# Two values of two products and two joined gates in the third blocks of batches 2 to 5

## The chip, the core and the metric

The kernel runs on one core of one Trainium2 chip. The core has a matrix engine (TensorE, PE in the profile), a vector engine (VectorE, DVE), a scalar engine (ScalarE, ACT), a general engine (GpSimd, POOL) and a queue engine for transfers (SyncE, SP). Each engine works through its own list of instructions in order; semaphores order the engines among each other. TensorE writes its products into PSUM, which here holds eight banks of 128 x 512 fp32. The metric is device time in microseconds (us) of one execution.

## The reference

For each of 8 batches of 3008 rows and 256 columns the real part of a two-dimensional Fourier transform is taken, and its rows go through a gated layer:

```python
X = np.fft.fft(x, axis=1)
X = np.fft.fft(X, axis=2)
x = X.real.reshape(B * S, D)
gate = np.maximum(x @ w_gate, 0.0)     # 256 -> 1536
val = x @ w_val                        # 256 -> 1536
out = gate * val @ w_out               # 1536 -> 256
```

## The kernel before, in words

**Mirror pairs.** The kernel folds the transform along the columns into the weights, and uses that the rows of a real transform come in mirror pairs. For a pair the gate (and the value) has the form A + B for the one row and A - B for its mirror. A is a product of the cosine parts `us` with WA, plus a term of channel 128 that is the same in both; B is a product of the sine parts `vs` with WB. Row 0 of `vs` carries channel 128 too, and row 0 of WB its weights. WM is -2 WB with row 0 set to zero, and `WV` is -0.5 WM, so WB with row 0 zero. Batch 0 is done in another way (`single_tile`, `first_tile`) that the change does not touch.

**Blocks, tiles and slots.** In batches 1 to 7 the pairs of a batch are cut into three blocks of 512, 512 and 481 columns (`thirds`, line 734). A block has 12 feature tiles of 128 features (fi = 0 to 11). One call of `slot` (line 1054) issues the work around one tile, `cur`; three further tiles are at earlier stages: `mid` (the next one), `nxt` (the one after it) and `after`. `pending` is the tile before `cur`. The slot whose `cur` is tile c is called slot c here; in it `pending` is tile c - 1, `mid` c + 1, `nxt` c + 2, `after` c + 3. The order of every engine's work is the order in which the kernel issues it (`manual_schedule`).

An ordinary tile goes through these steps:

- seed (`seed`, line 1014): ScalarE writes the channel 128 term of the gate into a p bank (two of them).
- sine and cosine of the gate (lines 1019 and 1026): TensorE makes -2B in the g bank, which ScalarE copies to q (line 1022), and adds the cosine product to the seed in the p bank, which gives A.
- `both` (lines 1030, 1031): VectorE makes A + B from q and the p bank; GpSimd then makes A - B from that and q. Both lie in SBUF, in buffers of tag r.
- value (`value`, lines 876 and 877): two products make A + B of the value in a v bank (two of them).
- first product (line 912, `relu_mult`): VectorE takes relu of the plus gate times the value and writes the first half of h.
- `mirror` (line 882): TensorE adds WM times `vs` to the same v bank, which turns it into A - B. It has to wait until VectorE has read the bank for the first product.
- second product (line 912, by `second`): VectorE makes the other half of h from the minus gate. For a block of 481 columns `keep_rest` (line 907) then copies 66 columns of h to `LB` by a DMA on the SP queue.

So an ordinary tile takes five products on TensorE and three operations on VectorE. The order inside a slot is, on TensorE: sine of `nxt`, some output products, cosine of `nxt`, mirror of `pending`, two value products of `cur`, more output products. On VectorE: second product of `pending`, first product of `cur`, `both` of `nxt`. On ScalarE: copy of q for `nxt`, seed of `after`, at most one eviction.

**Output products** (line 784) of the block before, 96 in a block of 512, fill the slots: `outs` of them in a slot, 8 in a third block, five eighths of them between sine and cosine and the rest behind the value. Every 24 of them make a PSUM bank full, which ScalarE copies out (line 797, the list `evict`: one entry of it is issued in each slot). **Transform products** (line 589) of the next batch go to the d bank during the first two blocks (`DFT_EVEN`). **Folds** of a later batch run on GpSimd, issued by a credit of 0.72 us in each slot (`run_fold`).

**Values of two products.** In the last third block of batch 6 and in batch 7 some tiles (`SHORT`, line 996) are marked `short`. For these ScalarE seeds the d bank with the channel 128 term of the value (`seed_value`, line 1035, at the end of the slot in which the tile is `nxt`). A slot later TensorE adds the cosine product (line 1039) and ScalarE copies twice that, 2A, to `a` (line 1040). A slot later again TensorE adds the sine product with `WV` (line 1044), so that the bank holds A + B, and VectorE makes the first product from it (line 912, reading d). In the slot after that VectorE takes 2A minus the bank, A - B, into `a` (line 1049) and GpSimd multiplies it by the minus gate (line 1050), on which ScalarE has done the relu (line 1103). There is no mirror product for such a tile. A `short` tile takes away two output products of the slot in which it is `mid` and adds one in each of the two slots after that.

**`widen`** (line 568) writes, by a product without a start flag, those columns of a bank that a transform product of 376 or 377 columns leaves out, so that a seed that ScalarE writes there is added to by the next product. It is issued for the transform of batch 7, which runs in batch 6. At batch 5, slot 0, a DMA on the SP queue (line 1210) sets row 0 of WB[0] to that of WM[0], zero.

Of the kernel before, what the change touches and what calls it, by code (L numbers as in the profile page):

```python
# [15 lines left out]
ALU = mybir.AluOpType  # L16
# [18 lines left out]
def kernel(  # L35
# [8 lines left out]
    nc = tc.nc  # L44
    B, S, D = x.shape
# [23 lines left out]
    WB = [single(f"WB{i}", [128, DF], BF16) for i in range(2)]  # L69
# [500 lines left out]
    def family(b, dst, fam, sine, now=True, pool=None):  # L570

        n, cols = (NE, slice(0, NE)) if fam == 0 else (NJ, slice(NE, NK))
        src, tab = (GG[b % 2], tabS) if sine else (FF[b % 2], tabC)
        st, apart = {}, now or pool is not None

        def mm(par, t, nyq=False):
            if par not in st and not apart and not par:
                st[0] = st[1]  # L580
            elif par not in st:
                home, tag = pool or ((psG, "g") if now and not par else (psD, "d"))
                st[par] = home.tile([128, 512], F32, name=tag, tag=tag)
            rows = slice(0, ROWS[par][t])
            if nyq:
                nc.tensor.matmul(st[par][0:1, 0:n], lhsT=FF[b % 2][rows, fam, t, par, 128:129], rhs=tabC[rows, 2 * t + par, cols],
                                 start=False, stop=(t == 2), skip_group_check=True)
            else:
                nc.tensor.matmul(st[par][:, 0:n], lhsT=src[rows, 1 - fam if sine else fam, t, par, 0:128],  # L589
                                 rhs=tab[rows, 2 * t + par, cols], start=(t == 0 and (apart or par == 1)), stop=(t == 2),  # L590
                                 skip_group_check=not apart)
                if (b, fam, sine, par, t) == (B - 1, 0, False, 0, 2):
                    widen(st[par], n)

        def end(par):
            if par:
                st["es"] = rp.tile([128, NE], F32, name="es", tag="es", bufs=2)
                evict.insert(0, lambda: nc.scalar.copy(st["es"][:, 0:n], st[1][:, 0:n]))
            elif not apart:
                whole, rest_ = half_of(dst, fam)  # L600
                evict.insert(0, lambda: nc.scalar.copy(whole, st[1][:, 0:n]))
                for c in (slice(0, NJ // 2), slice(NJ // 2, NJ)):
                    sums.append(lambda c=c: nc.vector.scalar_tensor_tensor(rest_[:, c], in0=st["es"][:, c], scalar=2.0, in1=st[1][:, c],
                                                                           op0=ALU.mult, op1=ALU.subtract))
            else:
                for d, op in zip(half_of(dst, fam), (ALU.add, ALU.subtract)):
                    m = d.shape[-1]
                    sums.append(lambda d=d, op=op, m=m: nc.vector.tensor_tensor(d, st["es"][:, 0:m], st[0][:, 0:m], op=op))
            if now:
                flush()  # L610

        def at(par):
            home, tag = pool
            st[par] = home.tile([128, 512], F32, name=tag, tag=tag)
            return st[par]
        return mm, end, at
# [242 lines left out]
    def run_one(todo):  # L859
        if todo:  # L860
            todo.pop(0)()
# [25 lines left out]
    def space():  # L887
        return rp.tile([128, 512], F32, name="r", tag="r", bufs=12)
# [26 lines left out]
    def second(st):  # L915
        (relu_mult if "s" in st else mult)(st, 1)
        if st["n"] == 481:
            keep_rest(st)
# [79 lines left out]
    def new_tiles():  # L998
        for b in range(1, B):
            for blk, block in enumerate(thirds):  # L1000
                for fi in range(NF):
                    st = tile_of(block, fi, uv[b])
                    st["b"] = b
                    st["kind"] = "o" if (b, blk, fi) == (1, 0, 6) else "n"
                    st["short"] = (b, blk) in ((6, 2), (7, 0), (7, 1)) and fi in SHORT or (b, blk) == (7, 2) and fi in (2, 5, 8)
                    st["lead"] = (b, blk, fi) == (1, 0, 0)
                    yield st

# [15 lines left out]
    def cosine_part(st):  # L1024
        n = st["n"]
        nc.tensor.matmul(st["p"][:, 0:n], lhsT=WA[0][:, st["f"]], rhs=st["us"], start=False, stop=True, skip_group_check=True)  # L1026

    def both(st):
        n, (q, sp, sm) = st["n"], st["s"]
        nc.vector.scalar_tensor_tensor(sp[:, 0:n], in0=q[:, 0:n], scalar=-0.5, in1=st["p"][:, 0:n], op0=ALU.mult, op1=ALU.add)  # L1030
        nc.gpsimd.tensor_tensor(sm[:, 0:n], sp[:, 0:n], q[:, 0:n], op=ALU.add)  # L1031

    def seed_value(st):
        st["v"] = bank("d")
        nc.scalar.activation(st["v"][:, 0:st["n"]], st["c"], ACTF.Copy, scale=b2[:, NF + st["fi"]:NF + st["fi"] + 1])
# [10 lines left out]
    def value_second(st):  # L1046
        n = st["n"]
        a = st["a"][:, 0:n]
        nc.vector.tensor_tensor(a, a, st["v"][:, 0:n], op=ALU.subtract)
        nc.gpsimd.tensor_tensor(half_h(st, 1), st["s"][2][:, 0:n], a, op=ALU.mult)  # L1050
        if n == 481:
            keep_rest(st)

    def slot(cur, mid, nxt, after, outs, fold_us):

        outs += cur["short"] + (pending is not None and pending.get("short", False)) - 2 * (mid is not None and mid["short"])
        stop = len(todo_out)

        def out(part):
            run(todo_out, len(todo_out) - stop + outs * part // 8)  # L1060
        old = nxt is not None and nxt["kind"] == "o"
        new = nxt is not None and nxt["kind"] == "n"
        if old:
            gate(nxt)
        lead = cur["lead"]
        out(4 if lead else 0)
        if new and mid["kind"] != "o":
            sine_part(nxt)
        out(4 if lead or nxt is None else 5)
        if new and mid["kind"] == "o":  # L1070
            sine_part(nxt)
        if new and not lead:
            cosine_part(nxt)
        if not lead:
            seed(after)
        if pending is not None and pending.get("short"):
            value_second(pending)
        elif pending is not None:
            mirror(pending["v"], pending, 1)
            second(pending)  # L1080
        if cur["short"]:
            value_sine(cur)
        else:
            value(cur)
        if mid is not None and mid["short"]:
            value_cosine(mid)
        if cur["kind"] == "o":
            mult(cur, 0, cur["first"])
        else:
            relu_mult(cur, 0)  # L1090
        if lead:
            out(5)
            cosine_part(nxt)
            seed(after)
        if new:
            both(nxt)
        if old:
            nxt["first"] = nxt["r"]
            mirror(nxt["g"], nxt, 0)
            relu(nxt)  # L1100
        if cur["short"]:
            sm = cur["s"][2][:, 0:cur["n"]]
            nc.scalar.activation(sm, sm, ACTF.Relu)
        if nxt is not None and nxt["short"]:
            seed_value(nxt)
        run_fold(fold_us)
        run_one(evict)
        run_one(sums)
        out(8)
        return cur  # L1110
# [4 lines left out]
    for b in range(B):  # L1115
# [4 lines left out]
        for blk, block in enumerate(blocks):  # L1120
# [72 lines left out]
            else:  # L1193
                for fi in range(NF):
                    at = NF * blk + fi
                    cur = ahead.pop(0)
                    add_h(cur, hs)
                    ahead.append(next(tiles, None))
                    outs = per_tile + ((-2, 0, -2, 2, 2, 0)[fi % 6] if per_tile == 7 else 0)
                    if (b, blk) == (B - 1, 2) and fi > 8:  # L1200
                        outs = (10, 9, 19)[fi - 9]
                        if fi == 9:
                            rest = out_steps(b, block, hs)
                            early, rest = rest[:10] + rest[12:16], rest[10:12] + rest[16:]
                            todo_out += early
                    if (b, at) in ((2, 5), (2, 9), (2, 13)):
                        f = slice(128 * (at - 5), 128 * (at - 1))
                        nc.scalar.mul(WV[:, f], WM[1][:, f], -0.5)
                    if (b, at) == (5, 0):
                        nc.sync.dma_start(out=WB[0][0:1, :], in_=WM[0][0:1, :])  # L1210
                    pending = slot(cur, *ahead, outs, .72)
                    for step in more_1.get(at, ()) if b == 1 else ():
                        step()
                    run(todo_dft, DFT_1[at] if b == 1 else DFT_EVEN[at])
# [44 lines left out]
```

## Time and profile before

| what | value |
|---|---|
| median of 3 runs | 626.28 us (626.09 to 626.63) |
| the profiled execution: time | 626.3 us |
| the profiled execution: span, first to last instruction | 624.5 us |
| mean granted TensorE clock | 0.999 of full speed |
| VectorE busy | 549.0 us (88%) |
| ScalarE busy | 464.3 us (74%) |
| GpSimd busy | 516.5 us (83%) |

A row of the timeline gives the start and the duration in us, the engine, the line and operation, and out<-in with partitions x elements; x3 means that three such instructions in a row are merged, and the duration is then from the start of the first to the end of the last. A bracket at the end tells how long the engine stood idle before it and what released it. Matmuls overlap: the next starts before the end of the one before is written, so what a product costs TensorE is the distance to the next start, not its duration.

### The profile page before, as it was taken

To read this page: it belongs to the slowest core of one execution; us is meant where nothing else is said; L and a number is where in the kernel's file an instruction comes from. 1 tells how busy PE (TensorE), PEld (TensorE's weight loads), DVE (VectorE), ACT (ScalarE), POOL (GpSimd) and SP (SyncE) were. 2 spreads that over 40 slices of the span, in tenths; PEclk is the share of its full clock that TensorE was granted. 3 is DMA by queue.
4 is the path that set the end of the run, shared out by engine and by line. 5 is a ranking of instruction groups with operands and counts; after the bars stand their busy time and mean duration, and the time that the engine had idled before them with its cause. 6 is when DMAs were issued, how large, how long until landed. Compare 5 with 4: busy or idle time off the path is not lost.

```text
span 624.5 us, 12395 instructions
## 1 busy us (share of the span) xinstructions
PE 615.7 (99%) x4047; PEld 397.1 (64%) x4091; DVE 549.0 (88%) x978; ACT 464.3 (74%) x854; POOL 516.5 (83%) x490
## 2 busy tenths in 40 slices
PE   8999999999999999999999999999999999999997
PEld 2566666566666666666666666666666666666666
DVE  8886677999899899988999999899999999999991
ACT  7796667777777767777777777777777768999982
POOL 8988992998899988799979989799896656888881
PEclk9999999999999999999999999999999999999999
DMA  9955758734264427315362425211211111211113
GB/s 241 212 199 132 176 186 105 186 64 143 86 153 141 133 70 198 101 48 163 85 189 66 138 77 127 57 52 51 77 47 52 43 61 37 61 52 51 44 52 104
DMA packets 86035, 66.48 MB, mean 106 GB/s; under 512 B 41639, under 2 KB 69063, under 8 KB 85970
## 3 DMA queue, kind: packets, MB, share of 16 engines
q1 hardware_dynamic: 81384, 60.02, 35.1%
q0 software_dynamic: 3984, 4.92, 4.0%
q8 instruction: 32, 0.52, 0.4%
q10 hardware_dynamic: 602, 0.75, 0.3%
q14 instruction: 33, 0.27, 0.1%
HBM read 41.89 MB, written 34.17 MB: 122 GB/s over the span
## 4 chain that ended last, share of the span: by engine, by line
PE 95%; DVE 1%; issue 1%; POOL 1%; DMA 1%; ACT 0%; DVEq 0%; POOLq 0%; ACTq 0%
PE o L784 38%; PE v L877 10%; PE v L882 10%; PE g L1019 9%; PE p L1026 8%; PE v L876 8%; PE d L589 4%; PE p L882 1%; PE p L876 1%; PE p L877 1%; DMA XG<-in_x_dram,gidx 1%; PE o L427 1%; POOL XG L120 1%; PE g L589 0%; DVE h L912 0%
## 5 line engine op out<-in xcount | busy, mean ns | idle before, releaser
L1031 POOL TENSOR_TENSOR r<-r 128x512 f32<-128x512 f32 (+1 forms) x251 | 312.6, 1253 | 84.3 <-DVE r L1030 83.1
L912 DVE SCALAR_TENSOR_TENSOR h<-r,v 128x512 bf16<-128x512 f32 (+1 forms) x478 | 303.5, 675 | 38.1 <-PE v L882 28.9
L784 PE MATMUL o<-wo,h 128*128 128x256 bf16 x2172 | 330.8, 272 | 0.2
L784 PEld LDWEIGHTS <-h 128*128 128x128 bf16 x2220 | 216.6, 98 | 111.5 <-issue 0.9
L1014 ACT ACTIVATE p<-CB,b 128x512 f32<-128x512 bf16 (+1 forms) x251 | 172.0, 685 | 62.3 <-DVE r L1030 61.2
L1022 ACT COPY r<-g 128x512 f32<-128x512 f32 (+1 forms) x251 | 144.8, 577 | 56.1 <-PE g L1019 51.0
L1030 DVE SCALAR_TENSOR_TENSOR r<-r,p 128x512 f32<-128x512 f32 (+1 forms) x251 | 168.5, 671 | 0.8 <-ACT r L1022 0.8
L877 PE MATMUL v<-V,WB 128*128 128x512 bf16 (+3 forms) x281 | 103.0, 367 | 2.1
L1019 PE MATMUL g<-V,WM 128*128 128x512 bf16 (+1 forms) x251 | 94.1, 375 | 0.2
L1026 PE MATMUL p<-U,WA 128*128 128x512 bf16 (+1 forms) x251 | 94.1, 375 | 0.0
L882 PE MATMUL v<-V,WM 128*128 128x512 bf16 (+1 forms) x240 | 89.9, 374 | 0.3 <-DVE h L912 0.2
L876 PE MATMUL v<-U,WA 128*128 128x512 bf16 (+3 forms) x245 | 89.3, 365 | 0.0
L901 DVE TENSOR_TENSOR h<-r,v 128x376 bf16<-128x376 f32 (+2 forms) x90 | 46.2, 547 | 16.4 <-PE v L882 10.5
L876 PEld LDWEIGHTS <-WA 128*128 128x128 bf16 x336 | 32.7, 97 | 37.3 <-issue 12.2
L797 ACT COPY os<-o 128x512 f32<-128x512 f32 x92 | 52.5, 571 | 2.9 <-issue 2.9
L877 PEld LDWEIGHTS <-WB 128*128 128x128 bf16 x336 | 32.7, 97 | 32.3 <-ACT WB L680 0.2
L198 POOL TENSOR_TENSOR XG<-XG,XD 128x510 f32<-128x510 f32 x42 | 52.8, 1268 | 0.5 <-DMA XG<-xr 0.5
L892 ACT ACTIVATE r<-p 128x376 f32<-128x376 f32 (+1 forms) x80 | 38.3, 486 | 18.0 <-PE p L882 8.6
L206 POOL TENSOR_TENSOR AA<-XG 128x510 f32<-128x510 f32 x42 | 45.3, 1090 | 0.0
L1019 PEld LDWEIGHTS <-WM 128*128 128x128 bf16 x251 | 24.6, 98 | 5.7 <-issue 0.3
L1026 PEld LDWEIGHTS <-WA 128*128 128x128 bf16 x251 | 24.5, 98 | 3.3 <-issue 0.2
L882 PEld LDWEIGHTS <-WM 128*128 128x128 bf16 x241 | 23.6, 98 | 2.9
(195 smaller groups left out, 478.3 us busy)
## 6 DMA issues: line engine op xcount, KB each, us to landing
out_dram<-os SPq DMA_DIRECT2D x124, 128.0 KB
xr<-in_x_dram SPq DMA_DIRECT2D x12, 768.0 KB
XG<-xr SPq DMA_DIRECT2D x12, 768.0 KB
XD<-in_x_dram SPq DMA_DIRECT2D x15, 512.0 KB
out_dram<-os SPq DMA_DIRECT2D x35, 112.0 KB
XD<-in_x_dram SPq DMA_DIRECT2D x8, 448.0 KB
CB<-ch SPq DMA_DIRECT2D x7, 376.2 KB
out_dram<-os SPq DMA_DIRECT2D x13, 96.0 KB
```

The lines of the kernel that those rows point to most:

```text
L198: e.tensor_tensor(XG[p, r, t, ::-1, 1:D], XG[p, r, t, ::-1, 1:D], XD[p, r, t, :, D - 1:0:-1], op=ALU.add)
L784: nc.tensor.matmul(st["p"][0:m, q, :], lhsT=lhs(f), rhs=wo[:, f, :], start=(f == 0 and not (early and q)), stop=(f == NF - 1), skip_group_ ...
L876: nc.tensor.matmul(bank[:, 0:st["n"]], lhsT=WA[i][:, st["f"]], rhs=st["us"], start=True, stop=False)
L877: nc.tensor.matmul(bank[:, 0:st["n"]], lhsT=WB[i][:, st["f"]], rhs=st["vs"], start=False, stop=True)
L882: nc.tensor.matmul(bank[:, 0:st["n"]], lhsT=W[i][:, st["f"]], rhs=v, start=False, stop=True, skip_group_check=True)
L912: nc.vector.scalar_tensor_tensor(half_h(st, sign), in0=st["s"][1 + sign][:, 0:n], scalar=0.0, in1=st["v"][:, 0:n], op0=ALU.max, op1=ALU.mult)
L1014: nc.scalar.activation(st["p"][:, 0:st["n"]], st["c"], ACTF.Copy, scale=b2[:, st["fi"]:st["fi"] + 1])
L1019: nc.tensor.matmul(st["g"][:, 0:n], lhsT=WM[0][:, st["f"]], rhs=st["vs"], start=True, stop=True)
L1022: nc.scalar.copy(q[:, 0:n], st["g"][:, 0:n])
L1026: nc.tensor.matmul(st["p"][:, 0:n], lhsT=WA[0][:, st["f"]], rhs=st["us"], start=False, stop=True, skip_group_check=True)
L1030: nc.vector.scalar_tensor_tensor(sp[:, 0:n], in0=q[:, 0:n], scalar=-0.5, in1=st["p"][:, 0:n], op0=ALU.mult, op1=ALU.add)
L1031: nc.gpsimd.tensor_tensor(sm[:, 0:n], sp[:, 0:n], q[:, 0:n], op=ALU.add)
```

## The change

In the third blocks of batches 2 to 5 (`mixed`):

- tiles 2 and 8 become `short`. Their minus value is made in another way than in the existing `short` tiles (`own`): VectorE writes 2A minus the bank back into the d bank, and `second` then makes the second product on VectorE from there, with its relu in it. GpSimd's multiplication and ScalarE's relu are not issued for them.
- tiles 5 and 11 get the kind "j". Their gate takes no g bank. In the slot in which the tile is `nxt`, TensorE adds only the cosine product to the seeded p bank and ScalarE copies twice that, 2A, to `sm`; no eviction is issued in that slot. In the next slot TensorE adds WB[0] times `vs` to the same bank (`add_sine`), ScalarE copies the sum A + B to `sp`, and GpSimd makes `sm` - `sp` = A - B. VectorE's `both` is not issued for them.
- a "j" tile moves two output products from the slot in which it is `mid` to the slot in which it is `nxt`.
- `widen` is issued for the transforms of batches 3 to 7, and row 0 of WB[0] is set to zero at batch 2, slot 0.

```diff
@@ family
-                if (b, fam, sine, par, t) == (B - 1, 0, False, 0, 2):
+                if b > 2 and (fam, sine, par, t) == (0, False, 0, 2):
                     widen(st[par], n)
@@ new_tiles
-                    st["kind"] = "o" if (b, blk, fi) == (1, 0, 6) else "n"
-                    st["short"] = (b, blk) in ((6, 2), (7, 0), (7, 1)) and fi in SHORT or (b, blk) == (7, 2) and fi in (2, 5, 8)
+                    mixed = 1 < b < 6 and blk == 2
+                    st["kind"] = "o" if (b, blk, fi) == (1, 0, 6) else "j" if mixed and fi in (5, 11) else "n"
+                    st["own"] = mixed
+                    st["short"] = mixed and fi in (2, 8) or (b, blk) in ((6, 2), (7, 0), (7, 1)) and fi in SHORT or (b, blk) == (7, 2) and fi in (2, 5, 8)
@@ new functions
+    def copy_cosine(st):
+
+        n, sp, sm = st["n"], space(), space()
+        st["s"] = sm, sp, sm
+        nc.scalar.mul(sm[:, 0:n], st["p"][:, 0:n], 2.0)
+
+    def add_sine(st):
+        n, (_, sp, sm) = st["n"], st["s"]
+        nc.tensor.matmul(st["p"][:, 0:n], lhsT=WB[0][:, st["f"]], rhs=st["vs"], start=False, stop=True, skip_group_check=True)
+        nc.scalar.copy(sp[:, 0:n], st["p"][:, 0:n])
+        nc.gpsimd.tensor_tensor(sm[:, 0:n], sm[:, 0:n], sp[:, 0:n], op=ALU.subtract)
@@ value_second
         a = st["a"][:, 0:n]
+        if st["own"]:
+            v = st["v"][:, 0:n]
+            nc.vector.tensor_tensor(v, a, v, op=ALU.subtract)
+            second(st)
+            return
@@ slot
+        joined, ready = (st is not None and st["kind"] == "j" for st in (nxt, mid))
+        outs += 2 * joined - 2 * ready
...
-        if new and not lead:
+        if ready:
+            add_sine(mid)
+        if (new or joined) and not lead:
             cosine_part(nxt)
+        if joined:
+            copy_cosine(nxt)
...
-        if cur["short"]:
+        if cur["short"] and not cur["own"]:
             sm = cur["s"][2][:, 0:cur["n"]]
             nc.scalar.activation(sm, sm, ACTF.Relu)
...
-        run_one(evict)
+        if not joined:
+            run_one(evict)
@@ loop over the tiles
-                    if (b, at) == (5, 0):
+                    if (b, at) == (2, 0):
                         nc.sync.dma_start(out=WB[0][0:1, :], in_=WM[0][0:1, :])
```

## The prediction

> **What bounds the kernel now.** I read the page first: busy shares, then the chain of waits.
>
> ```profile
> PE 615.7 (99%) x4047; PEld 397.1 (64%) x4091; DVE 549.0 (88%) x978; ACT 464.3 (74%) x854; POOL 516.5 (83%) x490
> ...
> PE 95%; DVE 1%; issue 1%; POOL 1%; DMA 1%; ACT 0%; DVEq 0%; POOLq 0%; ACTq 0%
> ```
>
> TensorE sets the end. What matters then is whether it also runs without a gap in the stage that is changed, and how near the other engines are to making one. The table of windows for most of the third block of batch 2 (window, length, then busy time of PE, PEld, DVE, ACT, POOL), and TensorE's waits between 110 and 520 us (us in total, times, longest):
>
> ```profile
> 228.00:247.00 19.00, 19.00 (x132) 12.78 (x131) 18.12 (x31) 13.89 (x24) 17.27 (x14) 1.00 0.60 145
> ```
>
> ```profile
> PE v L882 <- DVE h L912: 0.2, 1, 0.2
> ```
>
> TensorE has no gap there; VectorE is at 18.12 of 19.00 us. The one place where TensorE ever waits is the mirror product (L882), for VectorE's first product (L912). How near that wait is, one ordinary slot of this block shows (230.80 to the next sine product at 232.69):
>
> ```profile
> 230.80 0.37 PE L1019 MATMUL g<-V,WM 128*128 128x481 bf16 x1
> ...
> 231.00 0.71 PE L784 MATMUL o<-wo,h 128*128 128x256 bf16 x5
> ...
> 231.55 0.37 PE L1026 MATMUL p<-U,WA 128*128 128x481 bf16 x1
> ...
> 231.75 0.37 PE L882 MATMUL v<-V,WM 128*128 128x481 bf16 x1
> ...
> 231.96 0.37 PE L876 MATMUL v<-U,WA 128*128 128x481 bf16 x1
> ...
> 232.16 0.37 PE L877 MATMUL v<-V,WB 128*128 128x481 bf16 x1
> ...
> 232.23 1.23 DVE L912 SCALAR_TENSOR_TENSOR h<-r,v 128x481 bf16<-128x481 f32 x2
> 232.36 0.49 PE L784 MATMUL o<-wo,h 128*128 128x256 bf16 x3
> ...
> 232.69 0.37 PE L1019 MATMUL g<-V,WM 128*128 128x481 bf16 x1
> ...
> 233.37 0.65 DVE L1030 SCALAR_TENSOR_TENSOR r<-r,p 128x481 f32<-128x481 f32 x1
> ...
> 233.64 0.37 PE L882 MATMUL v<-V,WM 128*128 128x481 bf16 x1
> ```
>
> From start to start a product of 481 columns costs 0.204 us (231.75 to 232.36 for three), an output product 0.109 (231.00 to 231.55 for five); five and eight of them are 1.89 us, the slot. VectorE starts the second product of the pending tile 0.11 after the mirror has ended (231.75 + 0.37 to 232.23), ends the first product of the current tile at 233.46, and the next mirror, which overwrites the bank just read, goes at 233.64: a margin of 0.18. `both` comes behind the two products, so VectorE runs most of a slot behind TensorE: this `both`, at 233.37, belongs to the sine product of 230.80.
>
> **The change part by part.** The existing short tiles of batch 6, with the same 481 columns, are the nearest rows: their slots 1 to 4 around tile 2, and slot 5 for the second short tile.
>
> ```profile
> 521.76 1.26 DVE L912 SCALAR_TENSOR_TENSOR h<-r,v 128x512 bf16<-128x512 f32 x2
> ...
> 522.76 0.37 PE L1026 MATMUL p<-U,WA 128*128 128x481 bf16 x1
> ...
> 523.07 0.36 PE L882 MATMUL v<-V,WM 128*128 128x481 bf16 x1
> ...
> 524.54 0.57 ACT L1040 ACTIVATE r<-d 128x481 f32<-128x481 f32 x1
> ...
> 525.16 0.37 PE L882 MATMUL v<-V,WM 128*128 128x481 bf16 x1
> ...
> 525.37 0.37 PE L1044 MATMUL d<-V,kvec 128*128 128x481 bf16 x1
> ...
> 525.64 0.66 DVE L912 SCALAR_TENSOR_TENSOR h<-r,v 128x481 bf16<-128x481 f32 x1 [0.30 <-PE v L882]
> ...
> 526.01 0.37 PE L1019 MATMUL g<-V,WM 128*128 128x481 bf16 x1
> ...
> 526.21 0.65 DVE L912 SCALAR_TENSOR_TENSOR h<-r,d 128x481 bf16<-128x481 f32 x1
> ...
> 526.77 0.65 DVE L1030 SCALAR_TENSOR_TENSOR r<-r,p 128x481 f32<-128x481 f32 x1
> ...
> 527.34 0.65 DVE L1049 TENSOR_TENSOR r<-r,d 128x481 f32<-128x481 f32 x1
> ...
> 527.91 0.65 DVE L912 SCALAR_TENSOR_TENSOR h<-r,v 128x481 bf16<-128x481 f32 x1
> ...
> 528.76 0.37 PE L882 MATMUL v<-V,WM 128*128 128x481 bf16 x1
> ...
> 530.23 0.37 PE L1026 MATMUL p<-U,WA 128*128 128x481 bf16 x1
> ...
> 530.51 0.36 PE L882 MATMUL v<-V,WM 128*128 128x481 bf16 x1
> ```
>
> *Removed products.* A short value takes two products for three: 8 tiles, 8 x 0.204 = -1.63 us. A joined gate takes two as before, one of them a slot later: nothing. Output products are only moved; over slots 1 to 4 the shifts (-2, +1, +3, -2) add to zero.
>
> *Widening.* Four more of these:
>
> ```profile
> 514.34 0.22 PE L568 MATMUL d<-WB,WA 128*128 128x135 bf16 x1
> ...
> 514.40 0.38 PE L1019 MATMUL g<-V,WM 128*128 128x512 bf16 x1
> ```
>
> Each costs 0.06 to the next start; together +0.24.
>
> *The early mirror, slots 1 and 7.* With six output products the mirror of `pending` is due two of them (0.22) earlier in the slot, more than the margin of 0.18. In batch 6 it was due 0.204 after the cosine product at 522.76, so at 522.96, and went at 523.07, 0.05 after VectorE ended (521.76 + 1.26 = 523.02): a wait of 0.105. For the second short tile it is 530.23 + 0.204 to 530.51, 0.075. The changed slots 1 and 7 issue the same: (0.105 + 0.075) x 4 = +0.72. Bounds: nothing, if the first product were 0.1 earlier, to 0.22, the whole shift, in each of eight slots, +1.76.
>
> *The late mirror, slots 4 and 10.* In slot 3 VectorE loses the `both` of tile 5 and gains the write back, so it has three operations as before, and that looks balanced. But the order counts: the `both` stood last, behind the first product of tile 3, and the added subtraction stands first, ahead of it. The mirror of tile 3 in slot 4 waits for that first product. Take slots 2 and 3 of batch 6 as the clock. VectorE, from the mirror of tile 1 at 525.16: second product of tile 1 525.64, first product of tile 2 526.21, `both` of tile 4 526.77, subtraction 527.34. So far the same in the change. Then, where batch 6 has tile 3's first product at 527.91, the change has the second product of tile 2, which reads what the subtraction wrote. What such a dependence costs, three operations of the start show; the second reads the first one's output, the third does not depend on the second:
>
> ```profile
> 11.79 0.17 DVE L462 TENSOR_TENSOR AA<-XG,XD 128x8 f32<-128x8 f32 x1
> 11.99 0.43 DVE L441 TENSOR_TENSOR F<-AA 128x258 bf16<-128x258 f32 x1
> 12.34 0.42 DVE L439 SCALAR_TENSOR_TENSOR F<-AA 128x258 bf16<-128x258 f32 x1
> ```
>
> The dependent one starts 0.03 after the end of the one before, the other 0.08 before it. So tile 2's second product starts at 527.34 + 0.65 + 0.03 = 528.02, tile 3's first product 0.57 later at 528.59 and ends at 529.24; the mirror can go 0.05 after, at 529.29. TensorE would be there earlier: slot 3 begins at 526.01 and now has three products and eleven output products, 0.61 + 1.20 = 1.81, to 527.82; in slot 4 sine, three output products, `add_sine` and cosine come first, 0.94, so the mirror is due at 528.76. The wait is 0.53 us, in eight slots +4.24. Behind it in TensorE's queue stand the value products and then everything else; nothing overtakes. What VectorE saves by the missing `both` comes after this point, where it waits for the mirror of tile 3 (0.37 + 0.11) in any case, so it is no gain. The next mirror is due 1.89 after, and the recurrence that leads to it (0.37 + 0.11 + 0.57 + 0.65 + 0.05 = 1.75) fits again: one wait for each short tile.
>
> A subtraction that writes PSUM from VectorE is nowhere in the trace. The nearest rows are ScalarE's:
>
> ```profile
> L1035 ACT ACTIVATE d<-CB,b 128x481 f32<-128x481 bf16 x6 | 3.9, 647 | 0.0
> ...
> L1040 ACT ACTIVATE r<-d 128x481 f32<-128x481 f32 x6 | 3.4, 564 | 0.0
> ```
>
> Into the bank 647 ns, out of it 564. I take the subtraction's own 0.65 (L1049, the same inputs), since the engine is the nearer likeness; 0.083 more would be +0.66 in all, 0.083 less -0.66. Without the cost of the dependence (0.11) the wait is 0.42, -0.88 in all.
>
> The Trainium skill bears on that last term: its page "VectorE: DVE Perf Modes", section "The DRAIN you can't avoid", says that an operation starts only when the pipeline of the one before has emptied, and that a semaphore between the two costs nothing more. The trace disagrees by the 0.11 between the rows above. By the page's rule the wait would be 0.42 and the time 629.0 instead of 629.9.
>
> *ScalarE.* In a block: two seeds of a value (0.647), two copies of 2A (0.564), and one more copy for each joined gate (0.564 too): +3.5 us, where it had 5.1 idle in 19. In slots 0 to 2 it issues what batch 6 issues, except the relu, which falls away; there 2A was ready at 525.11 (524.54 + 0.57) and the sine product that overwrites the bank went at 525.37. So nothing on the path. If ScalarE were later by one seed (0.65), the sine product would wait 0.39, +3.1 in eight. The skipped eviction goes a slot later; its bank is next written when 24 more products have filled the other bank, three slots on.
>
> *GpSimd.* The number of subtractions is unchanged. That of a joined gate comes after ScalarE's copy in slot 4, about 1.6 us into it, where before it came after a `both` that ended at about the same time (the lag above); its reader, the second product in slot 6, is 5.2 us into slot 4. Its own time (us busy, mean ns) and a fold ahead of it are:
>
> ```profile
> L1031 POOL TENSOR_TENSOR r<-r 128x481 f32<-128x481 f32 x84 | 100.8, 1212 | 20.0 <-DVE r L1030 19.4
> ```
>
> ```profile
> 231.51 1.68 POOL L222 TENSOR_TENSOR G<-AA 128x762 bf16<-128x762 f32 x1
> ```
>
> 1.6 + 1.68 + 1.21 is 4.5, so it fits: nothing, and from about 0.7 us more on it would cost.
>
> *The DMA of row 0* moves three batches ahead on SP; no product has read that tile since the widening of batch 0, bar one gate tile in batch 1, and its reader comes two blocks later. Nothing.
>
> **The sum**, against the profiled execution's 626.3 (the median of the runs is 626.28, so nothing has to be shifted): -1.63 + 0.24 + 0.72 + 4.24 = +3.57, so 629.9 us.
>
> **The rivals.**
>
> *Late mirror not late.* VectorE's six operations between the mirrors of tiles 1 and 3 fit into TensorE's 3.60 us (525.16 to 528.76). For it: VectorE's count is balanced, and batch 6 with five operations shows no wait at 528.76. Against: six operations at 0.57 and the latencies make 4.13; they would have to take 0.53 less. Time: 626.3 - 1.63 + 0.24 + 0.72 = 625.6, not slower than before.
>
> *Only TensorE's count decides.* Neither mirror waits: 624.9. Against: the wait at 523.07 is in the trace.
>
> *The dependence is free*, the page's rule above: 629.0.
>
> *ScalarE late as well.* The value's sine product waits 0.39 in each of eight slots: 633.0. For it: ScalarE is the engine with the largest addition. Against: batch 6 runs the same order with 0.26 to spare.
>
> **How the numbers follow.** I give the forecast 0.72, the free dependence 0.08, the late mirror not late 0.08, TensorE alone 0.05, ScalarE late 0.07. The bounds of the forecast's own terms are -0.88 and -0.66 for the subtraction, -0.72 and +1.04 for the early mirror, +0.66 for the bank; not all fall one way, so I take about -1.6 to +1.2 for the forecast, 628.3 to 631.1. The range of 8 in 10 goes 0.7 beyond this on both sides towards the rivals, 627.6 to 631.8; it leaves out the two on the fast side and most of the last. About 0.2% (1.25 us) can be told from no change here; by that only 624.9 is faster, 625.6 is the same, the rest slower. With some room for a mixture: faster 0.06, same 0.08, slower 0.86.
>
> **What would show it.** TensorE's waits of the changed kernel should hold a row of L882's mirror for VectorE of about 4 to 5 us in all with a longest of about 0.5; in slots 4 and 10 of the third blocks of batches 2 to 5 the mirror should stand some 0.7 behind the start of the cosine product in place of 0.2, and in slots 1 and 7 some 0.3. The second product should start behind the end of the subtraction, not 0.08 before it. The value's sine product should not wait for ScalarE. If the mirror in slot 4 follows the cosine product at 0.2 us, the argument on VectorE's order is wrong; if the subtraction lasts 0.75 us, only its price is.

## The result, and the profile after

The changed kernel is slower: 630.84 us in the median of 6 runs (630.54 to 631.16) against 626.59 for the kernel before (626.09 to 627.20), a ratio of 1.0068 with a 95% interval of 1.0055 to 1.0081. The difference of the medians is +4.25 us, where +3.57 was forecast.

Three rows of the page after, busy time and the chain of waits, then TensorE's group for the mirror (times, busy us, mean ns, idle time before it):

```profile
PE 617.8 (98%) x4087; PEld 396.2 (63%) x4087; DVE 548.5 (87%) x978; ACT 474.0 (75%) x878; POOL 516.4 (82%) x490
...
PE 91%; DVE 5%; issue 2%; POOL 1%; DMA 1%; ACT 0%; DVEq 0%; POOLq 0%; ACTq 0%
...
L882 PE MATMUL v<-V,WM 128*128 128x512 bf16 (+1 forms) x232 | 86.9, 374 | 3.8 <-DVE h L912 3.8
```

VectorE still has 978 operations: the change is balanced in their number. Yet VectorE's share of the chain went from 1% to 5%, and the idle time stands in front of one kind of instruction, the mirror, released by the first product. TensorE's waits between 110 and 520 us say the same (us in total, times, longest):

```profile
PE v L882 <- DVE h L912: 3.8, 9, 0.5
```

Eight of these nine are new, one for each short tile. Slots 1 to 4 around tile 2 in batch 2, TensorE and VectorE (L1028 is the cosine product, L1032 `both`, L1065 the subtraction, L1043 the joined gate's second product; the line numbers have moved a little):

```profile
229.62 0.37 PE L1028 MATMUL p<-U,WA 128*128 128x481 bf16 x1
...
229.93 0.36 PE L882 MATMUL v<-V,WM 128*128 128x481 bf16 x1
...
232.02 0.37 PE L882 MATMUL v<-V,WM 128*128 128x481 bf16 x1
...
232.50 0.66 DVE L912 SCALAR_TENSOR_TENSOR h<-r,v 128x481 bf16<-128x481 f32 x1 [0.30 <-PE v L882]
233.07 0.65 DVE L912 SCALAR_TENSOR_TENSOR h<-r,d 128x481 bf16<-128x481 f32 x1
...
233.63 0.65 DVE L1032 SCALAR_TENSOR_TENSOR r<-r,p 128x481 f32<-128x481 f32 x1
...
234.20 0.66 DVE L1065 TENSOR_TENSOR d<-r,d 128x481 f32<-128x481 f32 x1
...
234.96 0.66 DVE L912 SCALAR_TENSOR_TENSOR h<-r,d 128x481 bf16<-128x481 f32 x1
...
235.21 0.37 PE L1043 MATMUL p<-V,WB 128*128 128x481 bf16 x1
235.41 0.37 PE L1028 MATMUL p<-U,WA 128*128 128x481 bf16 x1
235.53 0.65 DVE L912 SCALAR_TENSOR_TENSOR h<-r,v 128x481 bf16<-128x481 f32 x1
...
236.24 0.36 PE L882 MATMUL v<-V,WM 128*128 128x481 bf16 x1 [0.46 <-DVE h L912]
```

The mirror of slot 4 was due 0.204 after the cosine product at 235.41 and went at 236.24, 0.63 late. (The bracket says 0.46, since it counts from the end of the product before, which lasts 0.37 though the next could start after 0.204.) From 232.50 on VectorE waits for no other engine: it runs second product, first product, `both`, subtraction, second product of the short tile, and only then the first product that the mirror waits for, which ends at 236.18. In slot 1 the mirror went 0.31 after the cosine product instead of 0.204: 0.106 late. The second short tile of the block has 0.076 in slot 7 and 0.60 in slot 10 (the cosine product there has 512 columns, and the next product can start 0.217 after it):

```profile
247.26 0.38 PE L1028 MATMUL p<-U,WA 128*128 128x512 bf16 x1
248.08 0.36 PE L882 MATMUL v<-V,WM 128*128 128x481 bf16 x1 [0.44 <-DVE h L912]
```

The other three blocks show the same waits within about 0.01 us. TensorE's account of the change is: products removed -1.63, widening +0.24, early mirrors 4 x 0.18 = +0.7, late mirrors 4 x (0.63 + 0.60) = +4.9. The sum is +4.2, and +4.25 was measured.

### The profile page after: what moved, and what is told of

The parts are those of the page before. It is cut to its first block, busy times and chain, and to the rows that moved or that the text cites. A ratio compares the mean times of both kernels' runs of the same rounds, so it can differ in the third digit from the quotient of the medians.

```text
span 628.5 us, 12444 instructions
## 1 busy us (share of the span) xinstructions
PE 617.8 (98%) x4087; PEld 396.2 (63%) x4087; DVE 548.5 (87%) x978; ACT 474.0 (75%) x878; POOL 516.4 (82%) x490
## 4 chain that ended last, share of the span: by engine, by line
PE 91%; DVE 5%; issue 2%; POOL 1%; DMA 1%; ACT 0%; DVEq 0%; POOLq 0%; ACTq 0%
PE o L784 36%; PE v L882 10%; PE v L877 9%; PE v L876 9%; PE g L1021 8%; PE p L1028 8%; PE d L589 4%; DVE h L912 3%; PE p L882 1%; PE p L876 1%; PE p L877 1%; DMA XG<-in_x_dram,gidx 1%; DVE r L1032 1%; DVE d L1065 1%; PE d L1053 1%
## 5 line engine op out<-in xcount | busy, mean ns | idle before, releaser
L1033 POOL TENSOR_TENSOR r<-r 128x512 f32<-128x512 f32 (+1 forms) x243 | 302.9, 1253 | 84.9 <-DVE r L1032 82.8
L912 DVE SCALAR_TENSOR_TENSOR h<-r,v 128x512 bf16<-128x512 f32 (+1 forms) x462 | 294.0, 674 | 41.5 <-PE v L882 36.9
L1024 ACT COPY r<-g 128x512 f32<-128x512 f32 (+1 forms) x243 | 140.3, 578 | 50.3 <-PE g L1021 43.4
L1032 DVE SCALAR_TENSOR_TENSOR r<-r,p 128x512 f32<-128x512 f32 (+1 forms) x243 | 162.8, 670 | 0.8 <-ACT r L1024 0.8
L877 PE MATMUL v<-V,WB 128*128 128x512 bf16 (+3 forms) x276 | 101.2, 367 | 0.0
L876 PE MATMUL v<-U,WA 128*128 128x512 bf16 (+3 forms) x276 | 101.1, 366 | 0.0
L1028 PE MATMUL p<-U,WA 128*128 128x512 bf16 (+1 forms) x251 | 94.1, 375 | 0.0
L1021 PE MATMUL g<-V,WM 128*128 128x512 bf16 (+1 forms) x243 | 91.2, 375 | 0.2
L882 PE MATMUL v<-V,WM 128*128 128x512 bf16 (+1 forms) x232 | 86.9, 374 | 3.8 <-DVE h L912 3.8
L1021 PEld LDWEIGHTS <-WM 128*128 128x128 bf16 x243 | 23.8, 98 | 5.6 <-issue 0.3
L1028 PEld LDWEIGHTS <-WA 128*128 128x128 bf16 x251 | 24.5, 98 | 3.3 <-issue 0.2
L882 PEld LDWEIGHTS <-WM 128*128 128x128 bf16 x233 | 22.8, 98 | 3.6
```

What stands on the lines that cost most here:

```text
L876: nc.tensor.matmul(bank[:, 0:st["n"]], lhsT=WA[i][:, st["f"]], rhs=st["us"], start=True, stop=False)
L877: nc.tensor.matmul(bank[:, 0:st["n"]], lhsT=WB[i][:, st["f"]], rhs=st["vs"], start=False, stop=True)
L882: nc.tensor.matmul(bank[:, 0:st["n"]], lhsT=W[i][:, st["f"]], rhs=v, start=False, stop=True, skip_group_check=True)
L912: nc.vector.scalar_tensor_tensor(half_h(st, sign), in0=st["s"][1 + sign][:, 0:n], scalar=0.0, in1=st["v"][:, 0:n], op0=ALU.max, op1=ALU.mult)
L1021: nc.tensor.matmul(st["g"][:, 0:n], lhsT=WM[0][:, st["f"]], rhs=st["vs"], start=True, stop=True)
L1024: nc.scalar.copy(q[:, 0:n], st["g"][:, 0:n])
```

## The experiments

Theory, from the prediction: the loss is the place of two operations in VectorE's order. Rivals: the load itself (ScalarE's added copies, a VectorE operation that writes PSUM, GpSimd), the number of VectorE operations, and a cost of the joined gates. All medians are us; the ratio is to runs of the kernel before on the same chip, whose median was 626.32 beside `behind`, `sbuf`, `split` and `shorts`, 626.45 beside `joins`, `behind_shorts` and `best`, and 626.35 beside `between`.

| run | median | ratio (95%) |
|---|---|---|
| the change | 630.84 | 1.0068 (1.0055 to 1.0081) |
| `behind`: subtraction behind the first product | 625.54 | 0.9988 (0.9979 to 0.9997) |
| `sbuf`: difference kept in SBUF | 635.43 | 1.0144 (1.0128 to 1.0159) |
| `split`: mirror issued later in four slots | 628.90 | 1.0041 (1.0027 to 1.0055) |
| `shorts`: no joined gates | 630.48 | 1.0068 (1.0054 to 1.0082) |
| `joins`: only joined gates | 626.34 | 1.0001 (0.9992 to 1.0010) |
| `behind_shorts`: first repair, no joined gates | 630.91 | 1.0072 (1.0059 to 1.0086) |
| `best`: both repairs | 624.95 | 0.9976 (0.9966 to 0.9985) |
| `between`: as `best`, dependent operations apart | 624.73 | 0.9975 (0.9965 to 0.9984) |

### The order alone

```diff
-        if pending is not None and pending.get("short"):
+        behind = pending is not None and pending.get("short", False) and pending["own"]
+        if behind:
+            pass
+        elif pending is not None and pending.get("short"):
             value_second(pending)
...
             relu_mult(cur, 0)
+        if behind:
+            value_second(pending)
```

> The subtraction and the second product of the short tile are issued behind the first product of the current tile instead of ahead of it; nothing else is changed. If the order on VectorE makes the loss, the wait of 0.63 us of the mirror in slots 4 and 10 (eight in all, 4.9 us) is gone, the 0.11 and 0.08 in slots 1 and 7 stay, and the time is 630.8 - 4.9 = 625.9. If the loss comes from the load as such (ScalarE's additions, a VectorE operation that writes PSUM, GpSimd), the time stays within 0.5 of 630.8.

Measured 625.54. Slots 3 and 4 of batch 2 with this order:

```profile
233.59 0.65 DVE L1032 SCALAR_TENSOR_TENSOR r<-r,p 128x481 f32<-128x481 f32 x1
...
234.28 0.66 DVE L912 SCALAR_TENSOR_TENSOR h<-r,v 128x481 bf16<-128x481 f32 x1
...
234.86 0.66 DVE L1065 TENSOR_TENSOR d<-r,d 128x481 f32<-128x481 f32 x1
...
235.36 0.37 PE L1028 MATMUL p<-U,WA 128*128 128x481 bf16 x1
235.57 0.37 PE L882 MATMUL v<-V,WM 128*128 128x481 bf16 x1
235.62 0.66 DVE L912 SCALAR_TENSOR_TENSOR h<-r,d 128x481 bf16<-128x481 f32 x1
```

The first product now ends at 234.94 and the mirror follows the cosine product by 0.21, as in an ordinary slot. The same operations, with the same load on every engine, cost 5.3 us less as the medians stand, and 5.0 less (+4.25 to -0.78) when each is taken against the kernel before on its own chip; the eight waits were 4.9. That the load makes the loss is ruled out.

### The difference kept in SBUF

```diff
-            v = st["v"][:, 0:n]
-            nc.vector.tensor_tensor(v, a, v, op=ALU.subtract)
+            nc.vector.tensor_tensor(a, a, st["v"][:, 0:n], op=ALU.subtract)
+            st["v"] = st["a"]
             second(st)
```

> The difference is written into the SBUF buffer that holds 2A instead of back into the bank, and the second product reads it there. In the changed kernel the second product starts 0.10 us after the end of the subtraction, where the start of the kernel has 0.03 between dependent operations. If the 0.10 belongs to the PSUM bank, it falls to 0.03 here, the wait of the mirror in slot 4 from 0.63 to 0.56 and the time to 630.3. If any dependence on an operation of this length costs it, 0.10, 0.63 and 630.8 stay. If the write into PSUM is dear in itself, the subtraction gets shorter than 0.66.

Measured 635.43, which none of the three cases had foreseen. The subtraction is about as long as before, 0.65, so the write into PSUM is not dear; and the second product still starts 0.10 after its end (234.77 + 0.65 to 235.52 below), so the 0.10 does not belong to the bank. But the second product itself, now with both inputs in SBUF, takes nearly twice as long: 1.19 us in the mean of eight, against 0.65. Two of them, with GpSimd beside them:

```profile
233.88 2.36 POOL L1033 TENSOR_TENSOR r<-r 128x481 f32<-128x481 f32 x2
...
234.77 0.65 DVE L1064 TENSOR_TENSOR r<-r,d 128x481 f32<-128x481 f32 x1
...
235.52 1.24 DVE L912 SCALAR_TENSOR_TENSOR h<-r 128x481 bf16<-128x481 f32 x1
...
236.20 2.09 POOL L213 TENSOR_TENSOR F<-AA 128x768 bf16<-128x768 f32 x1
...
247.34 1.21 POOL L1033 TENSOR_TENSOR r<-r 128x481 f32<-128x481 f32 x1 [0.89 <-DVE r L1032]
247.93 1.13 DVE L912 SCALAR_TENSOR_TENSOR h<-r 128x481 bf16<-128x481 f32 x1
```

Each ends about 0.5 after GpSimd's running subtraction has ended (236.24 to 236.76, 248.55 to 249.06), as if most of it had waited for that. In the four blocks the first of the two is followed by a fold on GpSimd; it lasts 2.09 or 2.10 in place of the 1.68 that it takes in the change, where the second product reads PSUM. Two inputs in SBUF are not slow by themselves: the operations at 11.99 and 12.34 in the prediction have them too, and take 0.43 us for 258 columns while GpSimd only fills constants and issues a DMA; in proportion that is 0.8 for 481, an upper estimate. So the two engines hold each other up here. The Trainium skill states this, "SBUF — State Buffer", section "SBUF: two separate sides": a VectorE operation with two SBUF inputs and a GpSimd operation that reads SBUF take a shared pair of ports as a lock for the whole instruction. These rows agree with it, except that 0.5 is less than the 0.65 of a whole operation, which stays open. The change therefore writes the difference back into the bank with good reason: it keeps one input of the second product in PSUM.

### The mirror issued later

```diff
-        out(4 if lead or nxt is None else 5)
+        early = mid is not None and mid["short"] and mid["own"]
+        out(4 if lead or nxt is None else 7 if early or ready else 5)
```

> Same number of output products in each slot, but in slots 1, 4, 7 and 10 five of the six stand ahead of the cosine product, not three. The mirror is then due 0.22 later in them. By the order theory the waits in slots 1 and 7 (0.11 and 0.08) vanish and those in slots 4 and 10 fall from 0.63 and 0.60 to about 0.4: 0.75 + 8 x 0.22 = 2.5 less, 628.3. If TensorE is held by something else in these slots, the time stays at 630.8.

Measured 628.90. That is 1.9 less than the change as the medians stand, and 1.7 less when each is taken against the kernel before on its own chip; 2.5 was expected. Slot 4 of batch 2, then slot 5 of batch 4:

```profile
235.48 0.37 PE L1028 MATMUL p<-U,WA 128*128 128x481 bf16 x1
236.09 0.36 PE L882 MATMUL v<-V,WM 128*128 128x481 bf16 x1 [0.24 <-DVE h L912]
```

```profile
385.11 0.37 PE L1028 MATMUL p<-U,WA 128*128 128x481 bf16 x1
385.39 0.36 PE L882 MATMUL v<-V,WM 128*128 128x481 bf16 x1
```

The late mirror waits 0.41 as expected. What was missed is the slot after. With one output product left behind the value products instead of three, TensorE could go from mirror to mirror in 1.67 us (five products of 0.204 and six output products of 0.109), where the recurrence through VectorE in the prediction takes 1.75. So the mirror of slot 5 comes 0.28 after the cosine product, 0.076 late; in slot 11 it is 0.05. Over the eight slots this is 0.5 us, most of the difference to the expectation.

### What the joined gates give

Without them (all tiles of these blocks get the kind "n"):

```diff
-                    st["kind"] = "o" if (b, blk, fi) == (1, 0, 6) else "j" if mixed and fi in (5, 11) else "n"
+                    st["kind"] = "o" if (b, blk, fi) == (1, 0, 6) else "n"
```

> No joined gates: tiles 5 and 11 are ordinary, so VectorE has eight operations more (the sum for the gate), ScalarE eight copies fewer. The order theory: that operation comes behind the first product that the mirror waits for, and ends about when the mirror does, so the wait in slots 4 and 10 stays 0.6 and the time is 630.8 within 0.4. The rival, that the number of VectorE operations in the slot decides and the joined gates pay for the write back: 8 x 0.57 more, 635.4.

Measured 630.48. VectorE's eight added operations cost nothing in the place where they stand:

```profile
235.16 0.37 PE L1028 MATMUL p<-U,WA 128*128 128x481 bf16 x1
235.28 0.65 DVE L912 SCALAR_TENSOR_TENSOR h<-r,v 128x481 bf16<-128x481 f32 x1
235.85 0.65 DVE L1032 SCALAR_TENSOR_TENSOR r<-r,p 128x481 f32<-128x481 f32 x1
235.99 0.36 PE L882 MATMUL v<-V,WM 128*128 128x481 bf16 x1 [0.46 <-DVE h L912]
```

The `both` of tile 5 runs while VectorE would wait for the mirror of 235.99 in any case (235.99 + 0.36 + 0.11 is 236.46, and `both` ends at 236.50). The opposite run has only the joined gates:

```diff
-                    st["short"] = mixed and fi in (2, 8) or (b, blk) in ((6, 2), (7, 0), (7, 1)) and fi in SHORT or (b, blk) == (7, 2) and fi in (2, 5, 8)
+                    st["short"] = (b, blk) in ((6, 2), (7, 0), (7, 1)) and fi in SHORT or (b, blk) == (7, 2) and fi in (2, 5, 8)
...
-                if b > 2 and (fam, sine, par, t) == (0, False, 0, 2):
+                if (b, fam, sine, par, t) == (B - 1, 0, False, 0, 2):
```

> Only the joined gates; tiles 2 and 8 are ordinary and the widening is as before. TensorE has the same number of products as the kernel before, VectorE eight operations fewer, ScalarE eight copies more. The order theory: nothing that the mirror waits for is moved, 626.3 within 0.3. If the joined gates cost something by themselves (the skipped eviction, the copies on ScalarE, GpSimd later), the time is above 626.6.

Measured 626.34, no difference to the kernel before: they cost nothing either. With the order mended, though, they matter. The next run is `behind` without joined gates:

> The first repair without joined gates: slot 3 then has four VectorE operations in the order first product of tile 3, subtraction, second product of tile 2, sum for the gate of tile 5. The mirror of slot 4 no longer waits, but the second product of tile 3 comes about 0.7 us after that mirror has released it, and the mirror of slot 5 waits about 0.6 for the first product of tile 4: 625.5 + 8 x 0.6 = 630.1. If the order alone mattered and the joined gates gave nothing, as the run without them and without the repair suggests, 625.5.

Measured 630.91: without the joined gates the repair gives nothing. The time is near the expected 630.1, but two thirds of the wait stand in another place. TensorE's wait that is new, and slot 5 of batch 2:

```profile
PE p L1028 <- ACT p L1016: 2.1, 8, 0.3
```

```profile
236.00 0.65 DVE L1032 SCALAR_TENSOR_TENSOR r<-r,p 128x481 f32<-128x481 f32 x1
236.22 0.37 PE L1021 MATMUL g<-V,WM 128*128 128x481 bf16 x1
236.56 1.22 DVE L912 SCALAR_TENSOR_TENSOR h<-r,v 128x481 bf16<-128x481 f32 x2
236.68 0.67 ACT L1016 ACTIVATE p<-CB,b 128x481 f32<-128x481 bf16 x1 [1.06 <-DVE r L1032]
...
237.40 0.36 PE L1028 MATMUL p<-U,WA 128*128 128x481 bf16 x1 [0.27 <-ACT p L1016]
...
237.84 0.36 PE L882 MATMUL v<-V,WM 128*128 128x481 bf16 x1
```

The `both` of tile 5 is the fourth operation in its slot and ends at 236.65. The seed of tile 7 goes into the bank that it reads, so ScalarE can start it only at 236.68, and the cosine product waits for the seed: it goes at 237.40, where sine and five output products from 236.22 would end at about 236.97. The mirror behind it is 0.23 late as well, by VectorE (0.19 in slot 11). Together this is the 0.6 for each tile that was expected. So VectorE's number of operations does decide, but only once the operation that TensorE waits for stands first in its order.

### Both repairs

This run, `best`, has the order of `behind`, and the split of `split` for slots 1 and 7 only (7 eighths if `early`).

> Both orders mended: the subtraction and second product behind the current first product, and in slots 1 and 7 five of the six output products ahead of the cosine product. The order theory: no wait of a mirror that the kernel before does not have is left; the 0.75 us of slots 1 and 7 goes from the 625.5 measured for the first repair alone: 624.8, and 626.3 - 1.63 + 0.24 = 624.9 from the count of TensorE's products. If the waits in slots 1 and 7 come back elsewhere, 625.5.

Measured 624.95; TensorE's waits between 110 and 520 us are those of the kernel before:

```profile
PE v L882 <- DVE h L912: 0.2, 1, 0.2
```

In the last run, `between`, the first product goes between the subtraction and the second product instead of standing ahead of both (the lines are against `best`):

```diff
         if behind:
-            pass
+            v = pending["v"][:, 0:pending["n"]]
+            nc.vector.tensor_tensor(v, pending["a"][:, 0:pending["n"]], v, op=ALU.subtract)
...
         if behind:
-            value_second(pending)
+            second(pending)
```

> As the run with both repairs, but with the first product of the current tile put between the subtraction and the second product of the short tile, so that no operation of VectorE follows one whose output it reads. If the 0.10 us behind the subtraction is the price of that dependence, the next operation starts 0.57 after the start of the subtraction, not 0.76. If it is a price of a subtraction that writes the bank, whatever follows starts 0.76 after it. TensorE waits in neither case, by the first the first product ends 0.4 before the mirror is due, by the second 0.2; the time is 624.9, as with both repairs.

```profile
233.85 0.66 DVE L1105 TENSOR_TENSOR d<-r,d 128x481 f32<-128x481 f32 x1
234.42 0.65 DVE L912 SCALAR_TENSOR_TENSOR h<-r,v 128x481 bf16<-128x481 f32 x1
...
234.98 0.65 DVE L912 SCALAR_TENSOR_TENSOR h<-r,d 128x481 bf16<-128x481 f32 x1
235.06 0.37 PE L1028 MATMUL p<-U,WA 128*128 128x481 bf16 x1
235.27 0.37 PE L882 MATMUL v<-V,WM 128*128 128x481 bf16 x1
```

From the subtraction to the next operation it is 0.57, not 0.76: the extra 0.19 is the price of reading at once what was just written, and it is gone when one other operation stands between. The first product ends at 235.07, 0.2 before the mirror rather than the 0.4 that was expected; the 0.2 of the expectation's other case was too large by as much, so the 0.57 decides. The time, 624.73, cannot be told from 624.95. Both are below the kernel before, by 1.5 and 1.6 us (0.24% and 0.25%), close to the 1.39 of TensorE time that the change saves net of the widening.

## Why the prediction was right, step by step

- *Removed products, widening.* The prediction had -1.63 + 0.24 = -1.39. With all added waits taken out, `best` lies 1.5 below the kernel before on its chip (624.95 against 626.45). Right.
- *Early mirror.* The forecast took 0.105 and 0.075 from the short tiles of batch 6; batch 2 has 0.106 and 0.076. In `split` they are gone from these slots. `best` lies 1.50 below the kernel before on its chip and `behind` 0.78, so their removal gave 0.72, where 0.75 was expected. Right.
- *Late mirror.* The place, the cause and the chain are as forecast, and `behind` shows it by the order alone. The size was 0.53 and is 0.63 and 0.60. The step that is short is the price of the dependence: taken as 0.03 after the end of the subtraction from an operation of the start, it is 0.10 (234.86 to 234.96). Over eight tiles that is nearly 0.6 of the 0.7 us by which the sum was low. The other 0.3 between the forecast of 629.9 and the measured 630.84 is the kernel before, at 626.59 in the six runs where the sum started from 626.3.
- *The missing `both` gives nothing* in this order: `shorts` shows it. In the mended order it is worth over 5 us (`behind` -0.78, `behind_shorts` +4.46 against the kernel before), which the prediction didn't ask.
- *The subtraction that writes PSUM* takes 0.656 against 0.65 for the one into SBUF: the value taken in the middle of the range was right.
- *ScalarE, GpSimd, the moved DMA at nothing.* Between 110 and 520 us TensorE waits for none of them in the changed kernel, and `joins` costs nothing.

Apart from the late mirror, which was 0.7 short, every term came out within about 0.1 us of its forecast where a run tells it, so the total is not owed to errors that cancel. As to the rivals: that the late mirror is not late fell with the mirror at 236.24, and that only TensorE's products count fell with the wait at 229.93. That the dependence is free fell with 234.96 in the change, and `between` tried it directly: 0.76 from the subtraction to a dependent operation, 0.57 to an independent one. That ScalarE is late with 2A fell with the list of TensorE's waits, which holds only the mirror.

## What to carry to other kernels

Where an engine is at 95% in a stage, a balance of its operations is not enough: list what the engine that sets the time (here TensorE) waits for, and see whether an added operation stands ahead of that and a removed one behind it. An operation that others wait for goes first in its slot; what only fills a buffer goes behind it. Then count again, since the next limit in the queue, here the missing `both`, may only matter once the first is gone.

## What was not expected of the hardware

- A VectorE operation whose two inputs both lie in SBUF took 1.13 to 1.26 us beside a running GpSimd subtraction, against 0.65 with one input in PSUM, and a GpSimd fold right behind that subtraction took 2.09 us in place of 1.68 (`sbuf`).
- A VectorE operation that reads the output of the one just before it starts 0.10 after that one's end in the third blocks, whether the output is in PSUM or SBUF, but 0.03 after it at the start of the kernel. An independent one starts 0.08 before the end. Why the two dependent gaps differ was not tried.
